# Delta rule attention and a hash-routed MoE on one core: seven half-width products for eight in experts one to seven

## The chip, the cores and the metric

The kernel runs on one core of one Trainium2 chip. The metric is the device time of one execution in microseconds. TensorE (PE in the profile), VectorE (DVE), ScalarE (ACT), GpSimd (POOL) and SyncE (SP) each work through their own instructions in order. PEld is the weight load of TensorE, which can run beside its matmuls.

## The reference, cut to what matters

A delta rule runs over 768 steps for 4 batches of 8 heads of 48 dimensions. Its output is reshaped to 3072 tokens of 384 values, and each token goes through one of eight experts, chosen by a hash of its id:

```python
x = attn_out.transpose(0, 2, 1, 3).reshape(B * S, H * D)   # (3072, 384)
expert_idx = token_ids * 2654435761 % 8
for e in range(8):
    mask = expert_idx == e
    h = np.maximum(x[mask] @ w1[e], 0.0)    # w1[e]: (384, 1024)
    out[mask] = h @ w2[e]                   # w2[e]: (1024, 384)
```

All of it is float32. The change concerns the second part alone.

## The kernel before, in words

The first stage (lines 120 to 1126) computes the attention in chunks of 32 tokens. A planner (`order`, L229) with costs for each task fixes the order of its instructions on every engine. It writes the rows to `x_scratch` in DRAM, sorted by expert, and ends with the first product for 288 rows of the largest expert (`first["h"]`, L1116 to L1126).

The second stage (L1128 to L1284) goes through the eight experts, the largest first. Its order is the program order on each engine (`manual_schedule`, L1238). Expert e has room for `WIDTHS[e]` rows (424, 424, 392, 392, 380, 380, 366, 366), in `NBS[e]` blocks of `TB` = 32 rows. For expert 0 only `LATE` = 136 rows are left, since `EARLY` = 288 were done before.

- `fetch(e)` (L1145) loads the rows of e on SP's queue into `xs[e]`; `weights(e)` (L1230) loads `w1_sb` (128 x 3 x 1024, input row p·3+co) and `w2_sb` (128 x 8 x 384), 1.5 MB each, into one of three pool buffers, or for expert 4 into the buffer of expert 0.
- `turn(e, i)` (L1161) transposes the rows on VectorE in blocks of 32 into `xTs[e]`, with 3 blocks of 128 inputs; `places` (L1170) works out the rows to write to.
- `gemm1` (L1182) is the first product: for each of 8 blocks of 128 hidden units, three matmuls (the three blocks of inputs) with all columns (rows of the expert) add up in one PSUM bank of `hs_ps`. ScalarE or VectorE, in turns, applies the relu on the way to `h_sb`.
- `turned` (L1212) is the second product for one of 3 blocks of 128 outputs: eight matmuls over the hidden units, whose weights are every third column of w2 (`w2_sb[:, fo, i::CO]`), into a bank of `os_ps`; a VectorE transpose puts the result into `o_sb`. For expert 0 a contiguous copy of w2 (`w2_runs`) is used.
- `scatter` (L1222) writes a finished expert with one indirect DMA on POOL's queue per block of 32 rows.
- `direct` (L1196) is the second product of expert 7 with h as the weights, in three parts of 122 rows; each is copied to one of two `last_o` and scattered by one DMA.

For each expert the order is: first product, then for i = 0, 1, 2 `turn(e+1, i)` and `turned(e, i)`, then the scatters. `between` issues `fetch` and `weights` of later experts, on SP's queue alone. A loop for overflow (L1286) has no turns for these inputs.

One `matmul` of float32 shows as two records of PE and two of PEld.

## Time and profile before

| | us |
|---|---|
| median of 3 runs (lowest to highest) | 488.8 (487.79 to 496.54) |
| the profiled execution, whole | 486.72 |
| its span, first to last instruction | 485.1 |
| TensorE busy | 440.3 (91%) |
| VectorE busy | 249.5 (51%) |
| GpSimd busy | 175.0 (36%) |
| ScalarE busy | 170.5 (35%) |
| mean granted TensorE clock | 0.952 of full |

The profile is of one execution. A duration is that of one record; records of neighbouring instructions on one engine overlap, so the pace of a sequence is read from the starts. [...] The first stage takes the span up to about 221 us, the second the rest; the last instruction starts at 475.86 us, and the span ends at 485.1.

### The profile page before, as it was taken

What the parts mean: (1) busy time and instruction counts of PE and PEld (TensorE: products, weight loads), DVE (VectorE), ACT (ScalarE), POOL (GpSimd) and SP (SyncE); (2) the same over time, 40 slices, a digit from 0 to 9 for tenths busy, and PEclk for the clock granted to TensorE, in tenths of its full rate; (3) what the DMA queues carried; (4) which work ended last, traced back from release to release, by engine and by line L of the source; (5) the groups of instructions that cost most, each with busy time, mean ns of one, the idle gap of its engine ahead of it and who ended that gap; (6) DMA issues with size and microseconds to landing.
All of it is one profiled execution on the core that took longest, in us unless ns stands there. A gap on an engine that the chain in (4) does not pass through costs nothing. (4 is left out here: it accounts for less than half of the span.)

```text
span 485.1 us, 15906 instructions
## 1 busy us (share of the span) xinstructions
PE 440.3 (91%) x6544; PEld 335.5 (69%) x6544; DVE 249.5 (51%) x903; ACT 170.5 (35%) x361; POOL 175.0 (36%) x231
## 2 busy tenths in 40 slices
PE   6798898989988977789999999999999999999991
PEld 4675787877767876677896665766767767677650
DVE  6799899999999799981222121221212112121100
ACT  3569876858866566455000001001000010000100
POOL 9671323214131251532056007427054170541710
PEclk8759799989998899899999999999999999999997
DMA  8994646556573373544998237064090460000100
GB/s 128 148 154 110 113 86 131 108 102 122 105 133 83 97 163 80 106 168 114 317 311 251 94 59 282 22 201 157 10 321 29 100 255 3 24 23 7 38 32 16
DMA packets 98009, 58.28 MB, mean 120 GB/s; under 512 B 84262, under 2 KB 91953, under 8 KB 97168
## 3 DMA queue, kind: packets, MB, share of 16 engines
q1 hardware_dynamic: 88640, 39.67, 34.8%
q0 software_dynamic: 8016, 17.27, 13.2%
q8 instruction: 52, 0.85, 0.8%
q10 hardware_dynamic: 1280, 0.32, 0.3%
q14 instruction: 21, 0.17, 0.1%
HBM read 44.51 MB, written 10.65 MB: 114 GB/s over the span
## 5 line engine op out<-in xcount | busy, mean ns | idle before, releaser
L1224 POOL DMA_INDIRECT out_dram<-o_sb,idx x81 | 79.3, 979 | 123.1 <-DVE o_sb L1219 100.4
L1186 PE MATMUL h_ps<-xT,w_sb 128*128 128x392 f32 (+3 forms) x288 | 94.5, 488 | 0.0
L1189 ACT ACTIVATE h_sb<-h_ps 128x392 f32<-128x392 f32 (+4 forms) x32 | 14.9, 466 | 211.4 <-PE h_ps L1186 211.4
L1186 PEld LDWEIGHTS h_ps<-xT,w_sb 128*128 128x128 f32 x288 | 54.6, 190 | 38.2 <-issue 7.6
L1216 PE MATMUL o_ps<-h_sb,w_sb 128*128 128x392 f32 (+3 forms) x240 | 79.6, 491 | 0.0
L1216 PEld LDWEIGHTS o_ps<-h_sb,w_sb 128*128 128x128 f32 x240 | 60.3, 251 | 18.8 <-issue 0.2
L1191 DVE TENSOR_SCALAR h_sb<-h_ps 128x392 f32<-128x392 f32 (+4 forms) x32 | 16.9, 527 | 95.9 <-PE h_ps L1186 95.9
L700 POOL DMA_INDIRECT x_scratch<-x_sb,slot x24 | 25.9, 1078 | 104.1 <-ACT x_sb L695 34.1
L1219 DVE STREAM_TRANSPOSE o_sb<-o_ps 128x384 f32<-128x384 f32 (+4 forms) x24 | 16.1, 669 | 84.7 <-PE o_ps L1216 84.7
L571 DVE TENSOR_TENSOR U<-U,tmp 128x30 f32<-128x30 f32 (+9 forms) x180 | 58.1, 323 | 0.0
L567 DVE TENSOR_TENSOR tmp<-U,Ni 128x30 f32<-128x30 f32 (+9 forms) x180 | 57.9, 322 | 0.1
L602 PE MATMUL bank<-S,KQ 128*32 128x96 f32 x1472 | 38.6, 261 | 4.7 <-ACT S L748 4.0
L563 DVE SCALAR_TENSOR_TENSOR U<-U,Ni 128x1 f32<-128x1 f32 (+30 forms) x186 | 42.4, 228 | 0.2
L748 ACT ACTIVATE S<-psS 48x768 f32<-48x768 f32 x43 | 34.6, 806 | 19.0 <-PE psS L670 15.6
L602 PEld LDWEIGHTS bank<-S,KQ 128*32 128x32 f32 x1472 | 33.4, 117 | 8.7 <-ACT S L748 5.8
L670 PE MATMUL psS<-W,K 32*112 32x96 f32 x736 | 26.9, 275 | 8.7 <-ACT W L660 5.5
L641 PE MATMUL bank<-W,MT 64*64 64x48 f32 x768 | 30.3, 231 | 2.0 <-issue 1.5
L670 PEld LDWEIGHTS psS<-W,K 32*112 32x112 f32 x736 | 22.2, 178 | 12.1 <-ACT W L660 7.4
L641 PEld LDWEIGHTS bank<-W,MT 64*64 64x64 f32 x768 | 26.8, 145 | 4.9 <-issue 2.4
L506 POOL DMA_DIRECT2D Tz<-TU x24 | 17.6, 741 | 29.3 <-ACT Tz L951 12.7
L335 POOL DMA_DIRECT2D Q<-in_q_dram x40 | 23.0, 583 | 6.1 <-PE early L370 4.2
L489 ACT ACTIVATE MT<-GQ,kmask 128x256 f32<-128x256 f32 x48 | 22.3, 512 | 0.0
(167 smaller groups left out, 588.5 us busy)
## 6 DMA issues: line engine op xcount, KB each, us to landing
w_sb<-in_moe_w_dram SPq DMA_DIRECT2D x12, 1536.0 KB
V<-in_v_dram SPq DMA_DIRECT2D x96, 48.0 KB
K<-in_k_dram SPq DMA_DIRECT2D x89, 48.0 KB
Q<-in_q_dram SPq DMA_DIRECT2D x56, 48.0 KB
xr<-x_scratch SPq DMA_DIRECT2D x16, 145.5 KB
Tz<-TU POOLq DMA_DIRECT2D x24, 96.0 KB, 3.3
Q<-in_q_dram POOLq DMA_DIRECT2D x40, 48.0 KB, 4.4
w_first<-in_moe_w_dram POOLq DMA_DIRECT2D x3, 512.0 KB, 5.0
```

The costliest lines, as they stand in the source:

```text
L335: eng].dma_start(out=dst[quarter(b)],
L563: nc.vector.scalar_tensor_tensor(out=U[:, n, 0:n], in0=U[:, j, 0:n], scalar=Ni[:, j, n:n + 1], in1=U[:, n, 0:n], op0=ALU.mult, op1=ALU.add)
L567: nc.vector.tensor_tensor(t, U[:, j:n, 0:n].to_broadcast([P, m, n]), Ni[:, j, n + 1:, None].to_broadcast([P, m, n]), op=ALU.mult)
L571: nc.vector.tensor_tensor(U[:, n + 1:, 0:n], U[:, n + 1:, 0:n], t, op=ALU.add)
L602: nc.tensor.matmul(res[quarter(b), u], lhsT=KQ[:, u, a, quarter(b)], rhs=S0[:, b, u].rearrange("p r d -> p (r d)"), start=(a == 1 and u == ...
L641: nc.tensor.matmul(to[rows, h], lhsT=lhsT(rows, h), rhs=rhs[rows, h], start=(first and h == 0), stop=True, skip_group_check=True, tile_pos ...
L670: nc.tensor.matmul(late["S"][0:DP + D, b, 2 * D * u:2 * D * u + 2 * D], lhsT=K4[quarter(b), u].rearrange("p r d -> p (r d)")[:, 0:DP + D], ...
L700: put = nc.gpsimd.indirect_dma_start(out=x_dram[:, :], out_offset=bass.IndirectOffsetOnAxis(ap=slot[:, c:c + 1], axis=0), in_=x_sb.rearran ...
L748: put = nc.scalar.activation(S1[half(r), :, :, r], new[half(r), :, :, r], ACT.Copy)
L1186: nc.tensor.matmul(h_ps[:, :width], lhsT=w1_sb[:, co, fo * P:(fo + 1) * P], rhs=xT[:, co, :width], start=(co == 0), stop=(co == CO - 1))
L1216: nc.tensor.matmul(os_ps[i][:, 0:width], lhsT=w2_sb[:, fo, i::CO] if runs is None else runs[:, fo, i], rhs=h_sb[:, fo, 0:width], start=(fo ...
L1224: scat = nc.gpsimd.indirect_dma_start(out=out_q, out_offset=bass.IndirectOffsetOnAxis(ap=of[:, k:k + 1], axis=0), in_=o_sb[:, k], in_offse ...
```

## The change

For experts 1 to 7 the first product and for experts 1 to 6 the second product are written anew. Take two of the three 128-wide blocks of the inputs (of the outputs in the second product), the two halves of the hidden units and the two halves of the columns: a 2x2 by 2x2 block product. `seven1` and `seven2` compute it with seven products of half-width blocks for eight (Winograd's form of Strassen's product). The third block is multiplied as before. The sums of weight blocks (`sums_of_weights`) and of column blocks (`sums_of_columns`) that this needs, and the sums of partial results, are VectorE instructions; a partial result `al` goes through ScalarE.

- `seven1` goes through four blocks f, each of which makes two blocks of hidden units (f and f+4). `first(f)` issues five half-width matmuls and three VectorE sums, `second(f)` six half-width matmuls into the same two PSUM banks, two VectorE sums and three relus on ScalarE. The order is first(0), first(1), second(0), first(2), second(1), first(3), second(2), second(3). In between stand VectorE operations from `others`: the sums for the second product of the expert before (`sums2`), or for expert 1 the turns of rows of expert 2.
- `seven2` issues 16 half-width matmuls, the 8 of full width for the third block of outputs, and 12 of half width; results are collected in `oT` and transposed to `o_sb` by `turn_out`.
- The order of the stage changes: the first product of expert e+1 now stands between the first and the second product of expert e. `ready(e)` holds the turns of rows and `sums1(e)` and follows on the first product of expert e−1. `scatter` of an expert thus comes after the first product of the next, and the scatters of expert 6 directly before `direct`.
- Weights: the pool has two buffers for three, and the buffer of expert 0 serves experts 3 and 6. `fetch(e+2)` and `weights(e+2)` are issued after the second product of expert e−1.
- All eight PSUM banks are used in pairs in turn. `oT` is cleared at the start; the clearing of `os_ps` behind the narrowest width goes.

The diff, cut to its core:

```diff
-    with tc.tile_pool(name="w_pool2", bufs=3) as w_pool2, \
+    with tc.tile_pool(name="w_pool2", bufs=2) as w_pool2, \
...
+        banks = [ps_m.tile([P, BANK], F32, name=f"bank{i}") for i in range(8)]
+        os_ps, hs_ps, t_ps = banks[0:3], banks[3:6], banks[6]
+        HF, HB = F // 2, FO // 2
+        two = itertools.cycle([(banks[i], banks[i + 1]) for i in range(0, 8, 2)])
...
+        w2_runs = h_sums[:, 0:FO * CO * P].rearrange("p (o i d) -> p o i d", o=FO, i=CO)
...
+        def sums_of_weights(s, a11, a12, a21, a22):
+            return [lambda: plus(s[:, 0], a21, a22), lambda: minus(s[:, 1], s[:, 0], a11),
+                    lambda: minus(s[:, 2], a11, a21), lambda: minus(s[:, 3], a12, s[:, 1])]
...
+        def first_sums(pair, n, u):
+            al, be, de, ep = halves_of(pair, n)
+            nc.scalar.copy(part[u][:, 1, 0:n], al)
+            plus(part[u][:, 0, 0:n], part[u][:, 1, 0:n], be)
+            plus(part[u][:, 1, 0:n], part[u][:, 0, 0:n], ep)
+
+        def sums1(e):
+            w1 = w_tiles[e][0]
+            s = w1_sums
+            ops = sums_of_weights(s, w1[:, 0, 0:HF], w1[:, 1, 0:HF], w1[:, 0, HF:], w1[:, 1, HF:])
+            ops.append(lambda: minus(s[:, 4], w1[:, 2, 0:HF], w1[:, 2, HF:]))
...
+            for op in sums_of_columns([x_sums[:, i, 0:n] for i in range(4)], x[:, 0, 0:n],
+                                      x[:, 0, n:2 * n], x[:, 1, 0:n], x[:, 1, n:2 * n]):
+                op()
+
+        def seven1(e, h_sb, others):
...
+            def first(f):
+                al, be, de, ep = halves_of(used[f], n)
+                blk = slice(f * P, f * P + P)
+                mm(al, a(0, f), x[:, 0, 0:n], True)
+                mm(be, s[:, 1, blk], t[:, 1, 0:n])
+                mm(ep, s[:, 2, blk], t[:, 2, 0:n], True)
+                mm(de, s[:, 0, blk], t[:, 0, 0:n])
+                mm(de, a(2, f + HB), x[:, 2, n:2 * n])
+                first_sums(used[f], n, f % 2)
+                plus(h_sb[:, f + HB, n:2 * n], part[f % 2][:, 1, 0:n], de)
+
+            def second(f):
...
+                mm(al, a(1, f), x[:, 1, 0:n])
+                mm(al, a(2, f), x[:, 2, 0:n])
+                mm(ep, a(1, f + HB), t[:, 3, 0:n])
+                mm(ep, a(2, f + HB), x[:, 2, 0:n])
+                mm(de, s[:, 3, blk], x[:, 1, n:2 * n])
+                mm(de, s[:, 4, blk], x[:, 2, n:2 * n])
+                nc.scalar.activation(h_sb[:, f, 0:n], al, ACT.Relu)
+                plus(h_sb[:, f + HB, 0:n], part[f % 2][:, 0, 0:n], ep)
...
+            for f in range(HB + 1):
+                if f < HB:
+                    first(f)
+                    other(2)
+                if f:
+                    second(f - 1)
+                    other(2 if f == HB - 1 else 1)
+            other(len(others))
...
+        def seven2(e, h_sb, o_sb):
...
+            for f in range(HB):
+                mm(al, w2[:, f, 0::CO], h_sb[:, f, 0:n], f == 0)
+            for f in range(HB):
+                mm(be, s[:, 1, f], t[:, 1, f])
+            for f in range(HB):
+                mm(ep, s[:, 2, f], t[:, 2, f], f == 0)
+            for f in range(HB):
+                mm(de, s[:, 0, f], t[:, 0, f])
+            first_sums(pair, n, 0)
+            plus(oT[:, 1, n:2 * n], part[0][:, 1, 0:n], de)
+            for fo in range(FO):
+                mm(third[:, 0:2 * n], w2[:, fo, 2::CO], h_sb[:, fo, 0:2 * n], fo == 0)
+            nc.scalar.copy(oT[:, 2, 0:2 * n], third[:, 0:2 * n])
+            turn_out(e, o_sb, 2)
+            for f in range(HB):
+                mm(ep, w2[:, f + HB, 1::CO], t[:, 3, f])
+            for f in range(HB):
+                mm(de, s[:, 3, f], h_sb[:, f + HB, n:2 * n])
+            for f in range(HB):
+                mm(al, w2[:, f + HB, 0::CO], h_sb[:, f + HB, 0:n])
+            plus(oT[:, 1, 0:n], part[0][:, 0, 0:n], ep)
+            plus(oT[:, 0, n:2 * n], part[0][:, 0, 0:n], de)
+            turn_out(e, o_sb, 1)
+            nc.scalar.copy(oT[:, 0, 0:n], al)
+            turn_out(e, o_sb, 0)
...
+        def ready(e):
+            if e != 2:
+                turns_of_rows(e)
+            if e:
+                sums1(e)
...
+            hs = {0: m_h.tile([P, FO, CAP], F32, name="h_sb")}
+            gemm1(w1_sb, xTs.pop(0), hs[0], LATE)
+            ready(1)
+            for e in range(1, E):
+                hs[e] = m_h.tile([P, FO, CAP], F32, name="h_sb")
+                seven1(e, hs[e], sums2(e - 1, hs[e - 1]) if e > 1 else
+                       [lambda: turns_of_rows(2)])
+                xTs.pop(e)
                 if e + 1 < E:
...
+                    ready(e + 1)
+                h_sb = hs.pop(e - 1)
+                if e == 1:
                     for i in range(CO):
...
+                        turned(w2_sb, h_sb, o_sb, i, LATE, EB, w2_runs)
+                    scatter(idx[0], o_sb, range(EB, NBS[0]))
                 else:
...
+                    seven2(e - 1, h_sb, o_sb)
+                    scatter(idx[e - 1], o_sb, range(NBS[e - 1]))
+                if e + 2 < E:
+                    fetch(e + 2)
+                    weights(e + 2)
+            for kt in range(KT):
+                direct(w_tiles[E - 1][1], hs[E - 1], kt, LW, last_i[:, kt:kt + 1], True)
```

## Rows read from the trace of the kernel before

**Rows 1.** The page, part 1: busy us (share of the span), instructions.

```profile
PE 440.3 (91%) x6544; PEld 335.5 (69%) x6544; DVE 249.5 (51%) x903; ACT 170.5 (35%) x361; POOL 175.0 (36%) x231
```

**Rows 2.** Windows: from:to us, length, busy PE PEld DVE ACT POOL, clock, DMA, GB/s.

```profile
245.35:250.91 5.56, 5.56 (x50) 5.56 (x49) 1.47 (x5) 1.13 (x4) 3.59 (x4) 1.00 0.99 375
290.00:322.00 32.00, 32.00 (x99) 21.45 (x98) 6.39 (x11) 1.99 (x4) 13.71 (x14) 1.00 0.44 137
```

**Rows 3.** Timeline: start us, us, what; TensorE's products of experts 0 and 2.

```profile
245.35 5.72 PE L1186 MATMUL h_ps<-xT,w_first 128*128 128x136 f32 x48
...
250.91 5.72 PE L1216 MATMUL o_ps<-h_sb,w_runs 128*128 128x136 f32 x48
...
290.63 15.96 PE L1186 MATMUL h_ps<-xT,w_sb 128*128 128x392 f32 x48
...
306.43 15.96 PE L1216 MATMUL o_ps<-h_sb,w_sb 128*128 128x392 f32 x48
```

**Rows 4.** Weight loads, by line and shape (busy us, mean ns), then first starts.

```profile
L1216 PEld LDWEIGHTS o_ps<-h_first,w_first 128*128 128x128 f32 x48 | 11.6, 251 | 1.0 <-issue 1.0
...
L1186 PEld LDWEIGHTS h_ps<-xT,w_first 128*128 128x128 f32 x48 | 5.7, 190 | 0.1
...
233.53 0.25 PEld L1216 LDWEIGHTS o_ps<-h_first,w_first 128*128 128x128 f32 x1 [1.02 <-issue]
...
233.70 0.50 PEld L1216 LDWEIGHTS o_ps<-h_first,w_first 128*128 128x128 f32 x2
```

**Rows 5.** Timeline of VectorE operations, one beside a scatter; the last two strided.

```profile
174.88 1.04 POOL L700 DMA_INDIRECT x_scratch<-x_sb,slot  x1 [0.28 <-POOL x_sb L699]
...
175.66 0.67 DVE L555 TENSOR_TENSOR Ni<-NT,nd 128x496 f32<-128x496 f32 x1
176.25 0.56 DVE L513 TENSOR_TENSOR bank<-V,ntok 128x384 f32<-128x384 f32 x1
176.72 0.18 DVE L567 TENSOR_TENSOR tmp<-U,Ni 128x30 f32<-128x30 f32 x1
...
255.10 0.74 DVE L1166 STREAM_TRANSPOSE xT<-xr 128x448 f32<-128x448 f32 x1
...
255.76 0.14 DVE L1175 TENSOR_TENSOR idx<-xr,none_b 128x14 int32<-128x14 f32 x1
```

**Rows 6.** Timeline, VectorE's last relu of expert 0; a window, columns as rows 2.

```profile
251.11 0.30 DVE L1191 TENSOR_SCALAR h_sb<-h_ps 128x136 f32<-128x136 f32 x1 [1.09 <-PE h_ps L1186]
...
230.00:251.00 21.00, 20.40 (x110) 19.40 (x109) 4.53 (x13) 2.64 (x8) 3.68 (x4) 1.00 1.11 320
```

**Rows 7.** Windows of the first stage around two falls of the clock.

```profile
155.20:158.60 3.40, 3.40 (x40) 3.14 (x41) 3.40 (x14) 2.10 (x3) 0.00 (x0) 0.50 0.02 5
158.60:162.05 3.45, 3.45 (x70) 2.84 (x68) 2.56 (x12) 2.23 (x5) 1.99 (x3) 0.50 0.35 93
...
199.60:203.02 3.42, 1.89 (x60) 1.80 (x64) 3.20 (x14) 0.55 (x2) 2.21 (x3) 1.00 0.39 96
203.02:206.43 3.41, 3.41 (x76) 3.15 (x75) 2.75 (x14) 1.69 (x3) 2.23 (x5) 0.50 0.78 135
```

**Rows 8.** Timeline of the end, and landing times of L1224's scatters.

```profile
444.63 14.92 PE L1186 MATMUL h_ps<-xT,w_sb 128*128 128x366 f32 x48
...
445.81 0.98 POOL L1224 DMA_INDIRECT out_dram<-o_sb,idx  x1 [14.42 <-DVE o_sb L1219]
...
459.39 10.81 PE L1199 MATMUL o_ps<-w_sb,h_sb 128*122 128x384 f32 x33
...
459.93 0.98 POOL L1224 DMA_INDIRECT out_dram<-o_sb,idx  x1 [0.30 <-issue]
...
475.11 0.48 ACT L1203 COPY last_o<-o_ps 122x384 f32<-122x384 f32 x1 [9.83 <-PE o_ps L1199]
475.86 0.98 POOL L1205 DMA_INDIRECT out_dram<-last_o,last_i  x1 [4.07 <-POOLq L1286]
...
DMA to landing us min/median/max: 2.1/2.2/6.5
```

More of the change, by code (lines that the diff above doesn't have):

```diff
@@ new lines, in mm, with halves_of @@
+        def mm(out, lhsT, rhs, start=False):
+            nc.tensor.matmul(out, lhsT=lhsT, rhs=rhs, start=start, stop=True,
+                             skip_group_check=True)
+        def halves_of(pair, n):
+            ab, de = pair
+            h = BANK // 2
+            return ab[:, 0:n], ab[:, h:h + n], de[:, 0:n], de[:, h:h + n]
+        def first_sums(pair, n, u):
[3 more added lines that the diff above has]
+            plus(part[u][:, 1, 0:n], part[u][:, 0, 0:n], ep)
@@ new lines, in seven2 @@
+        def seven2(e, h_sb, o_sb):
+            w2, s, n = w_tiles[e][1], w2_sums, WIDTHS[e] // 2
+            t = h_sums[:, 0:4 * HB * n].rearrange("p (k f y) -> p k f y", k=4, f=HB)
+            pair, (third, _) = next(two), next(two)
+            al, be, de, ep = halves_of(pair, n)
+            for f in range(HB):
[23 more added lines that the diff above has]
+            turn_out(e, o_sb, 0)
@@ L1139, with turn_out @@
+        def turn_out(e, o_sb, i):
+            n = NBS[e]
+            nc.vector.transpose(o_sb[:, 0:n, i::CO],
+                                oT[:, i, 0:n * TB].rearrange("p (k t) -> p k t", t=TB))
         out_q = out.rearrange("n (q y) -> (n q) y", q=QN)
@@ L1241 @@
             weights(1)
+            ready(0)
             w1_sb, w2_sb = w_tiles[0]
-            for i in range(CO):
-                turn(0, i)
-            places(0)
             o_sb = m_o.tile([P, NB_MAX, DQ], F32, name="o_sb")
@@ L1256 @@
             n_ov = nc.values_load(ov_i[0:1, NOV:NOV + 1], min_val=0, max_val=NOV)
-            for e in range(E):
-                w1_sb, w2_sb = w_tiles[e]
-                def between(fo):
-                    soon = {(1, 0): 2, (1, FO - 1): 3}.get((e, fo), e + 2 if e > 1 and not fo else E)
-                    if soon < E:
-                        fetch(soon)
-                        weights(soon)
-                h_sb = m_h.tile([P, FO, CAP], F32, name="h_sb")
-                width = WIDTHS[e] if e else LATE
-                gemm1(w1_sb, xTs.pop(e), h_sb, width, between)
+            hs = {0: m_h.tile([P, FO, CAP], F32, name="h_sb")}
```

71 lines of the change are left out of this document (51 added, 20 removed).

## The prediction, made before the changed kernel ran

> **What bounds the kernel now.** I read the page's busy times first, then the windows by stage, then the timeline. TensorE (PE) is busy for 91% of the span [rows 1]. From 290 to 322 us, one expert in the middle of the second stage, PE is busy 32.00 of 32 us at full clock, VectorE (DVE) 6.39 and GpSimd (POOL) 13.71 [rows 2]. So here a microsecond of matmul taken away is a microsecond of span, and VectorE has some 25 us per expert to give.
>
> The price of a matmul comes from starts in the timeline, since the duration of one record overlaps its neighbour. One `matmul` of f32 is two records. 48 records of 392 columns go from 290.63 to 306.43, 329.2 ns each; 48 of 136 columns from 245.35 to 250.91, 115.8 ns each [rows 3]. The line through both is N/1.2 + 2.4 ns for N columns: the fixed part is tiny, so half the columns cost half the time, at full clock also among 136-column products [rows 2]. A weight load that took longer than this could spoil it: contiguous ones are recorded with 190 ns and still followed each other every 115.8 ns, so they hide [rows 3, 4].
>
> **The change part by part.**
>
> *TensorE.* Let n be half the width. A first product was 24 matmuls of 2n columns; `seven1` has 11 matmuls of n in each of 4 blocks, 44 or 88 records. That saves 48·(2n/1.2 + 2.4) − 88·(n/1.2 + 2.4) = 6.67n − 96 ns. `seven2` has 28 matmuls of n and 8 of 2n, 72 records, and saves 6.67n − 58 ns. For n = 212, 196, 196, 190, 190, 183, 183 (experts 1 to 7) the first products give 1.3+1.2+1.2+1.2+1.2+1.1+1.1 = 8.3 us, the second products of experts 1 to 6 give 7.4 us. Together 15.7 us.
>
> Off this go weight loads with a stride. 12 of the 28 half-width matmuls of `seven2` take every third column of w2, 24 records; the sums are contiguous. Such a load is recorded with 251 ns, but the first two in the trace start at 233.53 and 233.70, 0.17 us apart [rows 4]. With a floor of 165 to 168 ns, n = 196 (165.7 ns) loses nothing, n = 190 some 0.1 us and n = 183 some 0.3 us per expert: 0.5 us in all. If instead the whole 251 ns counts, it is 24·(251−166) = 2.0 us per expert and 12 us in all; I take the floor, because two starts stand in the trace. Gain: 15.2 us.
>
> *VectorE, does it hide?* A sum of 496 elements took 0.59 us from start to start, one of 384 0.47 [rows 5]: 0.06 us plus 1.07 ns per element. So 196 elements cost 0.27, 392 cost 0.48, 512 cost 0.61. With a 12-byte stride 448 elements took 0.66 us [rows 5]; 512 by this 0.75. For n = 196, beside a first product (88·165.7 ns = 14.6 us): 4·5 sums of partial results at 0.27 are 5.4, the `sums2` of the expert before 4·0.75 + 8·0.48 = 6.8, together 12.2 us. Beside a second product (14.6 us): three turns of rows 1.8, `sums1` 5·0.61 + 4·0.27 = 4.1, five sums 1.4, three transposes out 1.7, together 9.0. Both fit.
>
> Order matters too, as the queues are in order. In `seven1` the second half of a block waits for VectorE's three sums of its first half; between them on PE lies the first half of the next block. For block 0 the first half ends at 1.66 us (five matmuls of 0.33), VectorE starts 0.2 later, as the relu of 251.11 after the matmuls of 250.91 [rows 3, 6], and has two of the sums left (ScalarE's copy runs beside the later matmuls): 2.4 us, and PE asks at 3.3; for block 1 it is about 4.7 against 7.0. In `seven2` the first partial sums come behind the last block's tail (0.8), turns (1.8), `sums1` (4.1) and themselves (0.8), at about 7.5 us, and PE asks for them only after 16 half and 8 full matmuls, at 10.6. The next first product needs `sums1` 7 us after it is done. The slack is 0.9 to 3 us, so I cost all of it at nothing. If this cover is gone, see the second rival.
>
> [...]
>
> *The start.* Before, VectorE began the last relu of 136 columns at 251.11 [rows 6], by the price above 0.21 us, was free at 251.32 and turned expert 1's rows, while PE did `turned` for expert 0 from 250.91 on [rows 3]. Now `ready(1)` stands between `gemm1` of expert 0 and `seven1(1)`, and `turned` comes after `seven1(1)`. PE is done at 250.9 and finds on VectorE: three turns at 0.66, the places 0.15, five sums of weights at 0.61, two of rows at 0.29, before `be` of block 0 can run. 251.32 + 2.0 + 0.15 + 3.05 + 0.6 = 257.1. Only one matmul of 0.36 us fits in the hole (`al`). PE loses 257.1 − 250.9 − 0.36 = 5.9 us (5.5 to 6.5, by how a wait adds to each step). What DMA brings is not late: 320 GB/s from 230 to 251 us are 6.7 MB [rows 6], and expert 1's rows and 3.1 MB of weights stand first in that queue. The clearing of `oT` falls on VectorE into the wait before the relus.
>
> *The clock.* In the first stage PE's clock was at 1.2 GHz from 203.02 to 206.43, after 3.4 us in which PE was busy 1.89, and from 155.20 to 162.05 [rows 7]. A hole of 5.9 us will bring it down too. At half speed over 3.4 or 6.9 us of full work 1.7 or 3.4 us are lost; the least is 0, if the level holds. I take 1.9, near the shorter dip, as PE is packed afterwards.
>
> *The end.* Today expert 6's 12 scatters (445.81 to 459.93, one per 1.284 us) run under expert 7's first product, and the last of three `direct` scatters starts 475.86 − 459.39 = 16.5 us after the `direct` matmuls begin [rows 8]. Now `seven2(6)` stands right before `direct`. Its last transpose follows a ScalarE copy, so the first scatter starts about 1.6 us after `direct` begins (1.18 after the switch today [rows 8], plus that copy), and 12 of them hold the POOL queue until 1.6 + 15.4 = 17.0. The three `direct` scatters queue behind: 17.0, 18.3, 19.6. The third also needs `last_o[0]`, which the first frees only on landing (2.2 us [rows 8]): 19.2, copy 0.48, wait 0.3, so 20.0, or 21.1 if landing counts from the instruction's end. Cost 3.1 to 4.6 us; I take 3.8.
>
> *The rest.* Weights now live in three buffers for four. Loads for e+2 are queued once `seven2(e−1)` has read its buffer, a whole pair of products (29 us) before `sums1(e+2)`; hidden. `scatter` lags by one product, with 16 us of work in 29; hidden until the end.
>
> **Sum.** 15.2 − 5.9 − 1.9 − 3.8 = 3.6 us faster. The profiled execution took 486.7 us (span 485.1): 483.1. The runs shown (487.8, 488.8 and a stray 496.5) lie 1.1 to 2.1 above it; with 1.3 I forecast 484.4 us. Its own range, from the best ends (15.7, 5.5, 0, 3.1) to the worst (14.9, 6.5, 3.4, 4.6) and 0 to 2.1 for the runs: 479.6 to 488.4.
>
> **The rivals**, each as a run.
> - *Strided loads bind* (chance 0.08): the place is `seven2`, and it decides from a true load time above the 166 ns of a half-width record. 12 us more, 484.4 + 12 = 496, slower than before. For it speaks the recorded 251 ns, against it 233.53 and 233.70.
> - *VectorE falls behind inside `seven1`* (0.10): its quarter is 12.2/4 = 3.05 us against PE's 3.65; from 20% longer operations or waits on, PE waits in each block for partial sums stuck behind two interleaved weight sums (1.5 us, less 0.9 of slack). 0.6·4 blocks·6 experts = 14 us: 498.
> - *Half-width does not halve* (0.05): if the many waits between short matmuls cost half of the gain, 7.6 us, it is 492, no difference. The 136-column rows speak against it; they carry few waits.
> - *No hole at the start* (0.06): if VectorE could do expert 1's sums in its idle time before 251 (it was busy 4.53 of 21 us [rows 6]), hole and clock loss go: 476.6. Against it, all its queue is in program order.
> - *Scatters block VectorE* (0.03): each of the 12 `sums2` operations, which run while the scatters do, waits for some half of a 0.98 us scatter [rows 8]; 12.2 + 5.9 = 18.1 us against 14.6, 3.5·6 experts = 21 us: 505. The sum of 175.66 speaks against it [rows 5]. [...]
>
> **Chances.** Forecast 0.68. A measurement of this kernel can tell about 2% (9.8 us) from no change: faster than 479 are the fourth rival and a little of the forecast's own range, 0.09; slower than 498.6 the last and some of the first two, 0.10; within 0.81. The range leaves out the fourth and last rival and the upper half of the first two: 478.5 to 495.
>
> **What would show it.** Right: PE without holes from expert 2 on, first products of 392 columns in 14.6 us for 15.8, records of 196 columns every 166 ns; a hole of about 6 us near 251 that ends on VectorE's sums, then 1.2 GHz for a few us; a POOL chain at the end, with 15 scatters in a row. Wrong: holes between blocks that end on VectorE, loads of w2 more than 170 ns apart, a second product no shorter than before, or no hole at 251.

## The result, and the profile after

The changed kernel took 496.55 us (median of 20 executions, 492.55 to 502.15), the kernel before 490.31 (20, 486.14 to 496.54). The ratio is 1.0134, with a 95% interval of 1.0105 to 1.0163: slower by 1.3%, where 484.4 us was forecast, and above the range, which ended at 495. The profiled execution took 492.55 us with a span of 491.0, for 486.72 and 485.1 before; it was the fastest of the 20.

TensorE does have less to do. From part 1 of the page (answers to [rows 1]) and the windows, with one first product of 392 columns from 279.16 to 293.77 us (answers to [rows 2, 3]; columns as there):

```profile
PE 427.2 (87%) x6968; PEld 377.2 (77%) x6968; DVE 361.4 (74%) x1178; ACT 200.0 (41%) x463; POOL 182.4 (37%) x231
```

```profile
243.06:249.84 6.78, 5.72 (x49) 5.52 (x47) 2.52 (x7) 1.14 (x4) 4.50 (x5) 1.00 1.00 380
249.84:256.09 6.25, 0.63 (x2) 0.30 (x2) 6.18 (x13) 0.00 (x0) 5.03 (x5) 0.78 0.63 164
256.09:260.13 4.04, 4.04 (x11) 3.87 (x12) 1.68 (x6) 0.34 (x1) 0.89 (x3) 0.50 1.02 271
279.16:293.77 14.61, 14.61 (x90) 14.61 (x89) 12.50 (x30) 3.45 (x12) 5.05 (x5) 1.00 0.05 15
300.00:345.00 45.00, 44.73 (x232) 41.10 (x231) 32.41 (x75) 8.18 (x24) 17.54 (x17) 1.00 0.42 123
345.00:390.00 45.00, 41.42 (x230) 38.56 (x229) 31.16 (x72) 8.94 (x27) 23.56 (x23) 1.00 0.57 168
390.00:435.00 45.00, 42.86 (x231) 39.59 (x230) 34.63 (x81) 9.32 (x28) 14.91 (x14) 1.00 0.16 50
```

The fourth row is a first product: it takes the 14.6 us that were forecast for 15.8. The hole at the start is there (second row: PE busy 0.63 of 6.25 us), and behind it the half clock (third row: 0.50). What was not forecast stands in the last two rows: in the middle of the stage, where no hole was expected, PE lacks 3.6 and 2.1 us in 45.

All that stands ahead of the early second product of expert 0 (the attention and the first product of its 288 rows, which begins at 221.1 us in the profile of before) is the same code in every kernel here, and yet it lasts between 229.5 and 238.7 us from one execution to the next. So I compare the stretch behind it, read from the timeline: the stage runs from the first matmul of that second product to the first `direct` matmul, the tail from there to the start of the last scatter.

| kernel | stage, us | tail, us | median ratio to before |
|---|---|---|---|
| before, the profile above | 225.82 | 16.48 | 1 |
| changed, first profile | 230.45 | 20.35 | 1.013 |
| changed, `again` | 243.19 | 20.33 | 1.036 |
| changed, `again_b` | 221.09 | 20.35 | 0.998 |

(`again` and `again_b` are the same kernel, run again; see the experiments.) The profiled execution of `again_b` was a slow one (489.21 us, where the median was 485.64), but what it had too much lies ahead of the stage, which began at 237.30 us.

The tail is 3.9 us longer, as costed (3.8). Timeline of GpSimd, answering to [rows 8]; `direct` begins at 461.73:

```profile
463.25 0.98 POOL L1369 DMA_INDIRECT out_dram<-o_sb,idx  x1 [11.84 <-DVE o_sb L1281]
...
477.39 0.98 POOL L1369 DMA_INDIRECT out_dram<-o_sb,idx  x1 [0.30 <-issue]
478.68 0.98 POOL L1350 DMA_INDIRECT out_dram<-last_o,last_i  x1 [0.30 <-issue]
479.97 0.98 POOL L1350 DMA_INDIRECT out_dram<-last_o,last_i  x1 [0.31 <-issue]
482.07 0.98 POOL L1350 DMA_INDIRECT out_dram<-last_o,last_i  x1 [1.13 <-ACTq L1438]
```

The stage was to get 7.4 us shorter (15.2 less 5.9 and 1.9) and got 4.6 longer. The holes in its middle begin like this (timeline of the changed kernel, first product of expert 4):

```profile
352.16 0.81 PE L1163 MATMUL bank<-xT,w_sb 128*128 128x190 f32 x4
...
353.57 0.81 PE L1163 MATMUL bank<-xT,w_sums 128*128 128x190 f32 x4
...
354.21 1.56 PE L1163 MATMUL bank<-h_sb,w_first 128*128 128x196 f32 x8
...
356.80 0.62 DVE L1152 TENSOR_TENSOR h_sb<-part,bank 128x190 f32<-128x190 f32 x2 [2.90 <-remote]
...
358.96 0.33 ACT L1217 ACTIVATE h_sb<-bank 128x190 f32<-128x190 f32 x1 [1.00 <-remote]
...
360.35 1.32 PE L1163 MATMUL bank<-h_sums,w_sums 128*128 128x196 f32 x7 [0.67 <-issue]
...
360.42 0.62 DVE L1152 TENSOR_TENSOR h_sb<-part,bank 128x190 f32<-128x190 f32 x2 [2.05 <-remote]
```

The matmuls that start at 352.16 make the last block's `al`, done at 352.97; ScalarE's relu that waits for it (L1217) starts at 358.96, 6.0 us later. Those of 353.57 end the block at 354.38; VectorE's sum that waits for them starts at 360.42, 6.0 us later, and VectorE had nothing else to do for 2.05 us. TensorE had long gone on to the next product. The matmul was done, the waiting engine was idle, and the signal between them was missing: "remote" is what the profile writes where it finds no releaser. I call such a signal late. On time, a consumer starts 0.04 us behind the end of the matmul. (The end of a matmul is modelled in the trace and its start recorded; but at 360.42 TensorE had been issuing matmuls of the next product for 6 us.)

In this profile the ends of 62 of TensorE's 174 signalling matmuls from 225 us on have no recorded signal within 0.08 us; in the profile of before, none of 139. I call these ends unmatched. Not every one of them is a late signal: 36 of TensorE's signals are recorded at a time when no matmul ended (one more such signal, at the very end, stands in every profile), and the records of the rest are missing. VectorE and ScalarE have 84 and 35 unmatched ends here, but not one of their signals is recorded late, in this or in any other run: their records are missing, and the signals came (VectorE's sum that ended at 386.58 has no record, and the matmul that waits for VectorE started at 386.63). So it is TensorE's signals that are late. All stretches with unmatched ends are stretches with scatters on GpSimd.

TensorE is itself held up as well: before the start at 360.35 it stood still for 0.67 us, and the profile writes "issue", that is, it waited for nothing that the profile shows. From 300 to 435 us 2.9 of the 7.6 us of its holes stand before matmuls that wait for no signal.

### The profile page after: what moved, and what is told of

It is laid out like the page before. It is cut to its first block, busy times and chain, and to the rows that moved or that the text cites. A ratio compares the mean times of both kernels' runs of the same rounds, so it can differ in the third digit from the quotient of the medians.

```text
span 491.0 us, 17207 instructions
## 1 busy us (share of the span) xinstructions
PE 427.2 (87%) x6968; PEld 377.2 (77%) x6968; DVE 361.4 (74%) x1178; ACT 200.0 (41%) x463; POOL 182.4 (37%) x231
## 3 DMA queue, kind: packets, MB, share of 16 engines
q0 software_dynamic: 8016, 17.27, 13.4%
## 4 chain that ended last, share of the span: by engine, by line
PE 60%; DVE 11%; issue 11%; ACT 6%; POOL 4%; DMA 4%; another core or an unknown queue 2%; SPq 0%; POOLq 0%; DVEq 0%; ACTq 0%
PE bank L1163 26%; PE bank L641 8%; PE bank L602 6%; PE psS L670 4%; PE bank L1361 4%; POOL out_dram L1369 3%; PE pair L370 3%; PE pair L641 2%; DMA K<-in_k_dram 2%; DVE w_sums L1149 2%; PE pair L404 2%; PE bank L1331 1%; PE bank L1120 1%; ACT KQ L380 1%
## 5 line engine op out<-in xcount | busy, mean ns | idle before, releaser
L1163 PE MATMUL bank<-xT,w_sb 128*128 128x190 f32 (+3 forms) x200 | 43.7, 333 | 2.1 <-DVE h_sb L1336 2.1
L1152 DVE TENSOR_TENSOR h_sb<-part,bank 128x196 f32<-128x196 f32 (+3 forms) x84 | 27.2, 352 | 18.6 <-PE bank L1163 8.9
L1219 ACT ACTIVATE h_sb<-h_sb 128x392 f32<-128x392 f32 (+3 forms) x28 | 14.7, 526 | 61.2 <-issue 30.3
L1163 PE MATMUL bank<-x_sums,w_sums 128*128 128x196 f32 (+3 forms) x168 | 33.4, 336 | 4.6 <-DVE x_sums L1149 4.6
L1163 PEld LDWEIGHTS bank<-xT,w_sb 128*128 128x128 f32 x200 | 34.9, 193 | 2.6 <-DVE h_sb L1336 2.3
L1163 PE MATMUL bank<-h_sb,w_sb 128*128 128x380 f32 (+5 forms) x128 | 35.1, 419 | 0.3 <-issue 0.2
L1152 DVE TENSOR_TENSOR part<-part,bank 128x196 f32<-128x196 f32 (+3 forms) x68 | 24.1, 354 | 15.1 <-ACT part L1173 6.8
L1163 PEld LDWEIGHTS bank<-x_sums,w_sums 128*128 128x128 f32 x168 | 29.2, 197 | 5.0 <-DVE x_sums L1149 4.9
L1163 PEld LDWEIGHTS bank<-h_sb,w_sb 128*128 128x128 f32 x128 | 27.5, 255 | 5.5 <-issue 1.3
L1163 PE MATMUL bank<-h_sums,w_sums 128*128 128x196 f32 (+3 forms) x144 | 25.7, 330 | 1.8 <-issue 1.7
```

Of the source, the lines that this page charges most:

```text
L1152: nc.vector.tensor_tensor(out, a, b, op=ALU.add)
L1163: nc.tensor.matmul(out, lhsT=lhsT, rhs=rhs, start=start, stop=True, skip_group_check=True)
```

## The experiments

Runs of one group shared one chip and the runs of the kernel before. Unmatched ends and late signals are counted as above, without the one signal that every profile has; a "hole" is what the start of a record of TensorE lies behind its pace.

### First group: is it the scatters?

`again` is the changed kernel unaltered. In `noscat` the scatters of experts 1 to 5 go:

```diff
-                    scatter(idx[e - 1], o_sb, range(NBS[e - 1]))
+                    if e == E - 1:
+                        scatter(idx[e - 1], o_sb, range(NBS[e - 1]))
```

> The changed kernel once more, for a second look. Theory A (the scatters on GpSimd and the sums of two SBUF operands on VectorE get into each other's way, and while they run side by side the signals from one engine to the next come late): the same stretches as in the first profile (316 to 331, 347 to 361, 375 to 393 us) again show waits of VectorE and ScalarE on TensorE that end 1 to 6 us after the matmul, and TensorE again has holes of 6 to 9 us in all between 300 and 420 us. Theory B (an accident of one execution): the holes are elsewhere or gone, and the median of the fast runs is within 0.5% of the kernel before. By A the ratio to the kernel before is again 1.010 to 1.016.

> The scatters of experts 1 to 5 are left out, those of experts 0, 6 and 7 stay; so the output rows of five experts are not written. Theory A (scatters beside sums make signals late): no wait of VectorE or ScalarE on TensorE ends more than 0.1 us after the matmul between 300 and 430 us, TensorE's holes there shrink from 7.9 us to under 1.5, and the kernel is 5 to 9 us faster than the changed kernel. Theory C (the loads of weights and rows, or the fetch of instructions, make them late): holes and time stay within 2 us of the changed kernel.

`again` took 508.99 us for 490.26 before: 1.0362 (1.025 to 1.0475), more than the 1.010 to 1.016 expected. `noscat` took 485.76: 0.992 (0.987 to 0.997), 23 us less than `again` where 5 to 9 were expected. Windows of `again` and then of `noscat`:

```profile
300.00:345.00 45.00, 42.68 (x205) 38.01 (x204) 30.86 (x70) 7.33 (x21) 14.66 (x14) 0.96 0.33 98
...
390.00:435.00 45.00, 40.62 (x216) 38.36 (x214) 28.04 (x67) 7.70 (x24) 20.99 (x20) 0.92 0.26 87
```

```profile
300.00:345.00 45.00, 45.00 (x235) 42.08 (x234) 33.46 (x76) 8.06 (x24) 0.00 (x0) 1.00 0.31 85
...
390.00:435.00 45.00, 45.00 (x249) 42.45 (x248) 34.37 (x79) 7.89 (x24) 0.00 (x0) 1.00 0.12 36
```

POOL is empty in the second, PE full, and the stage is 221.56 us. Loads of weights and rows went on (85 GB/s), so theory C falls. The trouble was there in this execution too: 12 ends are unmatched and 6 signals late, all beside the scatters that are left (251 to 256, 286 to 291 and 467 to 473 us). So the scatters are needed for late signals. B falls too: the holes came back, larger. Part of their size is the clock: behind three holes of `again`, at 335.92, 363.22 and 397.36 us, the granted clock was 0.50 for 3.4, 3.4 and 6.8 us. That is up to 6.8 us of full speed lost (half of 13.6, an estimate for a packed TensorE), out of the 22.1 by which its stage is longer than that of `again_b`; in the first profile the clock stayed up in the middle of the stage.

In `start` the work of VectorE for expert 1 moves; in `end` the order at the end:

```diff
             for i in range(CO):
                 turned(w2_sb, first["h"], o_sb, i, EARLY, 0)
+                if i == 0:
+                    ready(1)
...
             gemm1(w1_sb, xTs.pop(0), hs[0], LATE)
-            ready(1)
```

```diff
+                if e == E - 1:
...
+                    for i in range(CO):
+                        turned(w_tiles[6][1], hs[6], o_sb, i, WIDTHS[6], 0)
+                    scatter(idx[6], o_sb, range(NBS[6]))
...
-                seven1(e, hs[e], sums2(e - 1, hs[e - 1]) if e > 1 else
+                seven1(e, hs[e], [] if e == E - 1 else sums2(e - 1, hs[e - 1]) if e > 1 else
                        [lambda: turns_of_rows(2)])
```

> The turns of rows and the sums of expert 1 stand behind the first block of the early second product instead of behind the first product of expert 0; the clearing of oT moves ahead of them. VectorE is free from 236 to 243 us. By the accounting of the first profile (hole of 7.0 us from 248.6 to 256.1, then 4 us at half clock, 2.0 us lost) the kernel is 7 to 9 us faster than the changed kernel, that is 0.982 to 0.986 of it and 0.995 to 1.000 of the kernel before. If instead the late signals of that stretch (VectorE's last relu 1 us late) make the hole, 5 us or more of it stay and the gain is under 4 us.

> Expert 6's second product goes back to eight products for seven, without sums, and stands before the first product of expert 7, so that its scatters run under that. By the accounting of the prediction (tail 3.8 longer, second product 1.1 longer) it is 2.0 to 3.5 us faster than the changed kernel. If the tail is hidden otherwise, it is 1 us slower.

`start` missed its 7 to 9 us: 503.65 us, 5.3 less than `again`, and as four executions of each spread over 6.8 and 7.6 us, even that is not clear. Holes of 2.8 and 2.1 us stay at 251 to 257, beside the first scatters. `end` missed as well: 517.87 us, 8.9 more than `again`. Its tail is short again (16.48), but now 24 scatters follow each other from 450.34 to 479.91, and VectorE waits 10.66 us for one signal inside expert 7's first product, where no sum of two SBUF operands is left:

```profile
467.07 0.35 DVE L1152 TENSOR_TENSOR part<-part,bank 128x183 f32<-128x183 f32 x1 [1.86 <-ACT part L1173]
...
478.08 0.35 DVE L1152 TENSOR_TENSOR part<-part,bank 128x183 f32<-128x183 f32 x1 [10.66 <-remote]
...
478.87 0.98 PE L1163 MATMUL bank<-x_sums,w_sb 128*128 128x183 f32 x2 [10.51 <-DVE h_sb L1152]
```

So theory A, which blamed the sums beside the scatters, could not be right as I had put it.

### Second group: sums, or the rate of TensorE's instructions?

`split` and `dummy` alter the kernel before, `paced` the changed one:

```diff
                 for co in range(CO):
+                    for at in range(0, width, width // 2):
+                        nc.tensor.matmul(h_ps[:, at:at + width // 2],
+                                         lhsT=w1_sb[:, co, fo * P:(fo + 1) * P],
+                                         rhs=xT[:, co, at:at + width // 2],
...
```

```diff
                 if between is not None:
                     between(fo)
+                    if width > P + 8:
+                        for _ in range(2):
+                            nc.vector.tensor_tensor(filler, w1_sb[:, 0, 0:BANK],
+                                                    w1_sb[:, 1, 0:BANK], op=ALU.add)
```

```diff
             for k in blocks:
+                if pause and k:
+                    for _ in range(2):
+                        nc.gpsimd.memset(filler, 0.0)
```

> The kernel before, with each matmul of the first products cut into two of half the columns: the same work, twice the records of TensorE for each microsecond, no sum added. The scatters run under the first products, as before. By TensorE's price per record (2.4 ns more for each) it costs 48 x 2.4 ns x 8 = 0.9 us. Theory A1 (it is the rate of TensorE's instructions beside the scatters that makes the signals late): the relus in the stretches with scatters wait 1 us and more beyond the end of their matmul, TensorE, which has three banks, waits for them in turn, and the kernel is 5 to 25 us slower than before. Theory A2 (it is VectorE's sums of two SBUF operands beside the scatters): no late signal, and within 1.5 us of before.

> The kernel before, with 16 sums of 512 elements from two SBUF operands on VectorE under each first product of experts 1 to 7, into a scratch tile that nobody reads. TensorE is left as it was. They take some 9.8 us of the 15.8 us of such a product. Theory A2 (sums of two SBUF operands beside scatters make signals late): relus wait 1 us and more beyond their matmul in the stretches with scatters, and the kernel is 5 to 25 us slower than before. Theory A1 (the rate of TensorE's instructions): no late signal, and within 2 us of before; scatters that meet a sum may be recorded with 1.2 to 1.4 us for 0.98.

> The changed kernel, with two clearings of a 128x512 tile on GpSimd (some 1.1 us by the 0.44 us of a 128x384 one) ahead of each scatter but an expert's first, so that scatters of experts 0 to 5 follow each other every 2.4 us for 1.285; the last ones (expert 6) are left. The 12 then take 28 us of the 29 us for an expert. The number of scatters and of sums stays the same. If what piles up is worked off between scatters (A1), late signals shrink to under 1 us, and the time comes near that without scatters: 0.99 to 1.00 of the kernel before. If each meeting of a scatter with a sum costs its own share (A2), as many are late as before, and the ratio stays at 1.01 to 1.04.

> The paced kernel with the early sums of expert 1 of the run before that moved them. By the accounting (hole of 7 us at the start, 2 us of half clock, both gone) it is 7 to 9 us faster than the paced one: 0.972 to 0.985 of the kernel before. If the late signals of the start are what makes the hole, and pacing does not help them, it is 3 us faster at most.

`split`: 524.61 us, 1.0725 (1.067 to 1.078). `dummy`: 0.9981 (0.995 to 1.002). So A2 falls: 9.8 us of sums per expert cost nothing. A1 stands in the main: with TensorE's matmuls cut in two, and not one sum added, 31 signals are late and the stage is 34.8 us longer than in the profile of before (some 6 of these are the halving itself, see `splitpaced`). Whether it is the number of matmuls, or the weight loads that double with them, these runs do not tell apart. And A1 expected no late signal in `dummy`, which has 11, with 25 unmatched ends; `plain`, below, shows that the kernel before has them without any sum. Timeline of `split`, relus of expert 2's first product:

```profile
309.29 0.57 DVE L1195 TENSOR_SCALAR h_sb<-h_ps 128x392 f32<-128x392 f32 x1 [5.18 <-remote]
...
317.06 0.50 ACT L1193 ACTIVATE h_sb<-h_ps 128x392 f32<-128x392 f32 x1 [11.10 <-remote]
...
317.61 4.29 PE L1187 MATMUL h_ps<-xT,w_sb 128*128 128x196 f32 x12 [4.23 <-ACT h_sb L1193]
```

`paced`: 492.04 us, 1.001 (0.997 to 1.005), on a chip where `split` shows late signals; its stage is 221.76, its windows from 300 to 435 us have PE at 45.00 of 45; 8 of its 177 ends are unmatched, and no signal is late. `startpaced`: 484.63 us, 0.9892 (0.984 to 0.994), 7.4 less than `paced`, as the accounting of the start has it; stage 212.83. Both ratios are above what was expected (1.00 at most, and 0.972 to 0.985). Both kernels pay for the pause at the end, which I had overlooked: expert 5's 12 scatters with two clearings are not through when expert 6's are ready, and the tail is 25.0 us for 20.35.

### Third group: the kernel before again, scatters without rows, and a version

`plain` is the kernel before. In `oob` the scatters of experts 1 to 5 take their index from a tile of `BIG`; `best` is `startpaced` with the old forms at the end, and without pauses in the last 24 scatters.

```diff
+                        for k in range(NBS[e - 1]):
+                            scat = nc.gpsimd.indirect_dma_start(
+                                out=out_q,
+                                out_offset=bass.IndirectOffsetOnAxis(ap=far[:, 0:1], axis=0),
...
```

```diff
+                if e == E - 1:
...
+                        turned(w_tiles[6][1], hs[6], o_sb, i, WIDTHS[6], 0)
+                    scatter(idx[6], o_sb, range(NBS[6]), False)
+                    gemm1(w_tiles[e][0], xTs.pop(e), hs[e], WIDTHS[e])
+                    break
```

> The kernel before once more, for a second profile of it. If the late signals belong to TensorE's rate of instructions, there are few or none from 290 us on, and TensorE has no hole above 0.3 us in its second stage. If they come with the chip and not with the change, they are here too, hidden by the three banks of the first product.

> The changed kernel, with the scatters of experts 1 to 5 left as instructions of GpSimd but with an index beyond the bound for every row, so that they write no rows; the output rows of five experts are not written. If the building of descriptors on GpSimd makes the signals late, the time stays that of the changed kernel, 1.012 to 1.040 of before, with TensorE's holes of 8 to 20 us between 300 and 430 us. If it is the packets that the scatters send (and what each of them reports), holes go under 2 us and the time comes to that without scatters, 0.987 to 0.997 of before.

> Early sums of expert 1, scatters of experts 0 to 4 paced, and at the end the old form for the second product of expert 6 and the first product of expert 7, in the order of the kernel before, so that the scatters of experts 5 and 6 run at full pace beside full-width products. By the accounting: 2.2 us more of TensorE, a tail 3.9 us shorter, 1.7 us faster than the paced kernel with early sums, that is 0.983 to 0.989 of the kernel before. If the tail of 3.9 us was hidden in other waits, it is 2 us slower than that one, 0.990 to 0.995.

`plain` has late signals too, 20, with 36 of 139 ends unmatched, and still PE at 45.00 of 45 us in all three windows from 300 on. Its first product has three banks, so a relu may be two blocks (4 us) late before TensorE notices. Only near 255 us, among the 136-column products, does it lose time, and the stage is 230.63 for 225.82. From its timeline there:

```profile
256.52 0.63 PE L1216 MATMUL o_ps<-h_sb,w_runs 128*128 128x136 f32 x4 [0.76 <-issue]
...
257.96 0.39 PE L1216 MATMUL o_ps<-h_sb,w_runs 128*128 128x136 f32 x2 [0.81 <-issue]
...
258.68 0.28 PE L1216 MATMUL o_ps<-h_sb,w_runs 128*128 128x136 f32 x1 [0.32 <-issue]
...
259.40 0.43 PE L1216 MATMUL o_ps<-h_sb,w_runs 128*128 128x136 f32 x2 [0.45 <-issue]
...
259.42 0.40 DVE L1219 STREAM_TRANSPOSE o_sb<-o_ps 128x160 f32<-128x160 f32 x1 [6.18 <-remote]
```

These matmuls end the third block of outputs. They add up in one bank, and all that they read the first block had read before, so there is nothing left for them to wait for; yet TensorE stops four times, for 3.0 us in all, and then runs 3.4 us at a granted clock of 0.50. Together that is the 4.8 us of the stage. So TensorE's own stops are not a consequence of a consumer that hears late. The half of the expectation that blamed the change alone was wrong: the kernel before has the trouble as well, hidden from 300 us on.

`oob`: 506.31 us, 1.031 (1.024 to 1.039), stage 240.20, with 41 late signals. Its queue has as many packets as before (8016) with fewer bytes (14.33 MB for 17.27). So it is not the writing of rows; whether it is the instructions on GpSimd (64 with this index) or the packets stays open, as both remained.

`best` missed: 491.78 us, 1.001 (0.998 to 1.004), above both its ranges, with 24 scatters without a pause again. From its timeline, expert 7's first product, now at full width:

```profile
452.63 0.54 DVE L1337 TENSOR_SCALAR h_sb<-bank 128x366 f32<-128x366 f32 x1 [14.26 <-remote]
...
453.23 3.59 PE L1332 MATMUL bank<-xT,w_sb 128*128 128x366 f32 x6 [7.09 <-issue]
...
460.35 0.84 ACT L1335 ACTIVATE h_sb<-bank 128x366 f32<-128x366 f32 x2 [16.38 <-remote]
```

Full-width matmuls put up with 12 scatters in a row, as in `plain`, and not with 24. I read this as something that piles up, more with a longer row and with more of TensorE's instructions in the same time, and that is worked off in pauses: the last of these signals came 3.7 us after the last of the 24 scatters had ended. What it is, no run shows.

### Fourth to sixth group: the pause or the hour?

`startpaced1` has one clearing for two; `splitpaced` is `split` with one clearing between scatters. The others are repeats.

> The paced kernel with early sums, with one clearing for two between scatters, so that they follow each other every 1.83 us for 2.32. If signals and scatters share a path of fixed capacity, overloaded at one scatter per 1.285 us and not at one per 2.32, a load in between gives holes in between: some holes of TensorE are back from 300 us on (2 to 10 us in all, for 25 back to back), and the time is 0.993 to 1.01 of the kernel before. If any pause between scatters lets the signals through, it is the time of the kernel with two clearings, 0.984 to 0.993.

> The changed kernel a third time, beside the paced ones on one chip. In the first two runs its ratio to the kernel before was 1.013 and 1.036, so the late signals are not of one size at all times. If they are there whenever scatters run back to back beside half-width products, the ratio is 1.01 to 1.04 again, with 8 us or more of holes from 300 us on. If they come and go with the chip and the hour, the changed kernel can come out at 1.00 to 0.99, and the paced kernels then differ from it by the start alone.

> Early sums and one clearing between scatters, beside the changed kernel. If the pause does it, 0.975 to 0.993 of the kernel before, 2.5% or more under the changed kernel beside it, and no hole of TensorE above 0.5 us from 300 us on. If its run before was short only because no signal was late at that time in any kernel, it lies with the changed kernel, less the 9 us of the start: 0.99 to 1.02.

> The kernel before with each matmul of the first products cut into two of half the columns, and one clearing between scatters: no sum and no block product in it. If late signals come from TensorE's rate of instructions beside scatters without a pause, the 7% of the run without the pause go: 1.000 to 1.012 of the kernel before. If the half-width matmuls themselves cost the time, it stays at 1.06 or more.

> The kernel before with the matmuls of its first products halved, once more (1.0725 in its first run). If the signals are on time in this execution, only the half-width matmuls are left to pay, as in the run with a pause between scatters: 1.005 to 1.015 of the kernel before. If they are late, 1.04 to 1.09, with holes of TensorE that end on ScalarE's or VectorE's relus.

> Early sums and one clearing between scatters, once more. If the signals are on time in the kernels beside it, 0.975 to 0.990 of the kernel before. If they are late there, a pause of one clearing is enough when this is 0.984 to 0.994 with no hole above 0.5 us from 300 us on, and too short when it is 0.995 or more with such holes.

> One look at the changed kernel beside these two, to see whether its signals are late: by the first runs 492 to 510 us with holes of 8 us and more from 300 us on if they are, 481 to 490 us and none if they are on time.

| group | kernel | ratio to before (95% interval) | unmatched ends of TensorE | late signals |
|---|---|---|---|---|
| 4 | `startpaced1` | 0.983 (0.976 to 0.990) | 0 of 175 | 0 |
| 5 | `again_b` | 0.998 (0.994 to 1.001) | 0 of 179 | 0 |
| 5 | `startpaced1_b` | 0.985 (0.978 to 0.991) | 0 of 175 | 0 |
| 5 | `splitpaced` | 1.010 (1.004 to 1.017) | 0 of 122 | 0 |
| 6 | `split_b` | 1.059 (1.051 to 1.067) | 37 of 124 | 31 |
| 6 | `startpaced1_c` | 0.968 (0.963 to 0.973) | 27 of 173 | 1 |
| 6 | `again_c` (one execution, 512.27 us) | 1.04 by 493.7 | 63 of 180 | 43 |

Late signals come and go. In the fifth group there were none, and there the unaltered changed kernel is level with the kernel before; but that group ran on a chip that no other group used. The fourth ran on the chip of the first, and its one profile has no unmatched end, where the same kernel has 27 in the sixth; the kernel before took 486.66 us there, and 490.26 in the first group. So it seems to change on one chip, though the unaltered changed kernel was not run in that group. In the sixth group, on the chip of the third, late signals were there. One clearing was enough: 27 ends unmatched, but one signal late, beside the last scatters, which have no pause, and no hole from 300 us on; the time is below the 0.984 to 0.994 expected. Windows of `startpaced1_c`, then its scatters, one per 1.7 to 2.0 us:

```profile
300.00:345.00 45.00, 45.00 (x258) 43.60 (x257) 37.05 (x86) 10.94 (x34) 33.82 (x43) 1.00 0.65 189
345.00:390.00 45.00, 45.00 (x244) 42.52 (x244) 34.37 (x80) 8.62 (x26) 28.24 (x36) 1.00 0.38 106
390.00:435.00 45.00, 45.00 (x266) 43.17 (x265) 35.15 (x84) 11.17 (x35) 33.01 (x44) 1.00 0.17 57
```

```profile
312.59 0.98 POOL L1373 DMA_INDIRECT out_dram<-o_sb,idx  x1 [0.16 <-issue]
313.57 0.54 POOL L1372 MEMSET filler<- 128x512 f32 x1
314.27 1.24 POOL L1373 DMA_INDIRECT out_dram<-o_sb,idx  x1 [0.17 <-issue]
315.51 0.55 POOL L1372 MEMSET filler<- 128x512 f32 x1
```

Its stage is 212.75 us, that of the first two 212.77 and 212.90: it no longer depends on the hour. The tail is 20.35 again, as one clearing lets expert 5's scatters finish in time. `startpaced1` (early sums of expert 1, one clearing between scatters) beats the kernel before in all three groups, and the changed kernel in the two in which that ran beside it. In the fifth it is 1.4% under the changed kernel (478.8 for 485.64), less than the 2.5% expected, as no signal was late there and the early sums alone could pay. `splitpaced` against `split_b` is not a clean pair, as they ran in groups with and without late signals; it shows what halved matmuls cost by themselves. Its stage is 6.3 us longer than that of before. But 5.1 of these stand in the first product of expert 0, which was cut to 68 columns: 96 records from 241.26 to 251.93 us, one per 111 ns, for 48 of 136 columns at 116 ns. The seven products that were cut to 183 to 212 columns together take 1.1 us more in 109. The theory that each time between 1.285 and 2.32 us from scatter to scatter gives holes in between was wrong: at 1.7 to 2.0 us there were none.

## Why the prediction was wrong, and where it was right

**The step that failed** is the one that costed VectorE at nothing: "The slack is 0.9 to 3 us, so I cost all of it at nothing". It rested on VectorE starting "0.2 later" than its matmul, from one row. In the first profile of the changed kernel TensorE's signals took up to 6 us while scatters ran. `seven1` and `seven2` send TensorE's partial results through VectorE and back with 0.9 to 3 us to spare, where the relus of before had 4; each late signal first delays the sums, then the turns and `sums1` behind them in the queue, and TensorE stops in `seven2` (a hole of 1.6 us behind 366.45: the second half of `ep` may not be added before VectorE has read the first). Its end, from the timeline of the changed kernel:

```profile
368.39 1.71 PE L1163 MATMUL bank<-h_sums,w_first 128*128 128x196 f32 x8 [1.45 <-DVE oT L1152]
```

TensorE's stops with nothing to wait for, 2.9 of 7.6 us there, had no term in the sum at all. The stage of the first profile is 9.4 us longer than in `again_b` (230.45 less 221.09), and that alone is more than the 6.2 us between the two medians. What makes TensorE's signals late stays open; that it takes scatters without a pause is shown by `noscat`, `paced` and `startpaced1_c`. That the trace of before had no late signal, and that I had one execution of it, hid this: `plain` shows them.

**With signals on time the sum nearly held.** In `again_b` the changed kernel is 1.2 us faster by its ratio (0.9976, and the interval takes in 1), for 3.6 forecast. Its stage is 4.7 us shorter, its tail 3.9 longer, and 0.4 us are gained behind it. By terms:
- The matmuls' price was right: 161 and 166 ns for records of 190 and 196 columns.
- Strided weight loads were mis-sized, and their rival's 251 ns was further off. The floor is 174 ns, not 165 to 168, which is past the 170 that was to be a sign of being wrong: in `again_b` 48 such records of 196 columns and 48 of 190 both follow each other every 173.8 ns, 24 of 183 every 172.9. That is 24·8 ns for each of experts 2 and 3, 24·13 for 4 and 5, 24·18 for 6: 1.4 us for 0.5.
- The hole was 6.0 us in `again_b` (1.24 + 4.75), as costed (5.9); 7.0 in the first profile, since VectorE's last relu came 1 us late (249.84). The granted clock was 0.50 for 4.0 us of full work, 2.0 us for 1.9 (the windows show a share of the full clock and no frequency, so the prediction's 1.2 GHz stands for this half). `startpaced` gave both back: its stage is 8.9 us shorter than that of `paced`.
- The tail was 3.9 for 3.8.
- Some 1.5 us are left (15.7 less 1.4, 6.0, 2.0 and the 4.7 of the stage), for which I had no term; nine gaps of about 0.1 us inside first products make 0.9 of them.

**The rivals.** "VectorE falls behind inside `seven1`" named the right place, and 498 us is near what was measured, but that is luck, as its cause was another: VectorE's operations are about as long as costed (512 elements every 0.60 us, with a stride 0.77 to 0.88 for 0.75), and without scatters it keeps up. "No hole at the start" was wrong for this order of the work; `startpaced` shows that moving the sums ahead closes the hole. "Scatters block VectorE" was wrong in the engine that pays; its wait of half a scatter for each sum was an estimate that no run shows. What the runs show is a longer scatter beside a sum of two SBUF operands. In `again_b` the scatter of 317.78, begun during a sum, took 1.30 us for 0.98:

```profile
316.49 0.98 POOL L1369 DMA_INDIRECT out_dram<-o_sb,idx  x1 [24.95 <-DVE part L1152]
317.78 1.30 POOL L1369 DMA_INDIRECT out_dram<-o_sb,idx  x1 [0.30 <-issue]
```

```profile
317.37 0.85 DVE L1152 TENSOR_TENSOR w_sums<-w_sb 128x512 f32<-128x512 f32 x1
318.25 0.86 DVE L1149 TENSOR_TENSOR w_sums<-w_sums,w_sb 128x512 f32<-128x512 f32 x1
```

No sum grew by it (sums with a stride have records of 0.85 us in `noscat` too, without scatters), while 28 of the 29 scatters longer than 1 us from 245 us on in `again_b` meet such a sum. And `dummy`, which has 16 such sums under every first product from expert 1 on, is level with before. "Half-width does not halve" is wrong for the widths used: `again_b` has the gain, and `splitpaced` puts the cost of halving at 1% of the products from 366 columns up. It is right further down: the price line N/1.2 + 2.4 ns gives 59 ns for 68 columns, and 111 were measured.

## What to carry to other kernels

A partial result that goes from TensorE to another engine and back needs slack for its signal (up to 6.0 us late in the first profile) and not only for the work: look in the trace at how long after its matmul a waiting instruction really starts, where indirect DMAs run, and in more than one execution. Slack does not cover all of it, since TensorE also stops by itself (3.0 us in `plain`). Indirect DMAs in a long row on GpSimd, beside a dense stream of short TensorE instructions, are better spread out; a filler of 0.54 us between two of them and sums issued early made 35 us of difference where signals were late (`startpaced1_c` against `again_c`), twice what the saved products are worth. Compare stage by stage, since the stretch before the change alone moved by 9 us between executions.

## What the hardware did that I had not expected

TensorE's signals came up to 6 us late in the first profile, and VectorE waited 10.66 us for one in `end`, while scatters followed each other every 1.285 us; with 1.7 to 2.0 us from start to start none was late, and without scatters there was none in the stretch. VectorE's and ScalarE's signals were late in no run. Late signals come with scatters in a row, and they do not need the rows that the scatters write (41 in `oob`). The longest waits stand where TensorE issues twice as many matmuls beside the scatters (an idle time of 11.10 us before a relu in `split`, for 6.54 at most in `plain`, some 3.4 us of each being usual there) and where the row is longest (16.38 us in `best`). In the same stretches TensorE stops with nothing to wait for (0.32 to 0.81 us idle before four matmuls in `plain`), and records of signals are missing for three engines (26 of TensorE's, 84 of VectorE's and 35 of ScalarE's in the first profile), also where pauses keep all signals but one on time (26 of TensorE's in `startpaced1_c`). The trouble was there in some groups and not in others (43 late signals in `again_c`, none in `again_b`). The shared thing behind it was not found, and the profile names it only as "remote" and "issue". No run here shows whether an execution that records nothing has late signals.
